# Inputs transposed by the DMA, and a convolution operand kept block by block, in a fused attention and state-space kernel

## The chip, the core and the metric

The kernel runs on one core of a Trainium2 chip. The core has five engines with queues of their own: TensorE (PE in the profile; PEld is its weight loads), VectorE (DVE), ScalarE (ACT), GpSimd (POOL) and SyncE (SP, which here only issues transfers). Sixteen DMA engines move data. The metric is the device time of one execution in microseconds.

## The reference

The inputs are x (2048 rows, 448 columns), the projections, and the parameters of a state-space layer (448 channels, 256 states), all in bf16. Two layers read the same x and a gate mixes them:

```python
q = (x @ wq).reshape(B, S, 16, 28).transpose(0, 2, 1, 3)
k, v = x @ wk, x @ wv                       # one K/V head for all 16 query heads
p = softmax(einsum("bhqd,bkd->bhqk", q, k) * 28**-0.5)
a = einsum("bhqk,bkd->bhqd", p, v) -> (B, S, 448) @ wo

dt = exp(log_dt)[:, None]                   # state-space layer, A, B, C complex
K[d, l] = Re( sum_n C[d,n] * exp(dt*A[d,n]*l) * dt*B[d,n] )      # l = 0..2047
b = causal convolution of x with K, per channel, + x * Dskip

g = sigmoid((x * gate_w).sum(-1, keepdims=True))
out = g * a + (1 - g) * b
```

## The kernel before

Every piece of work is an operation with an engine, an estimated duration, the data it reads and writes, and a priority `pr`. A planner (`Prog.schedule`, L158) simulates the engines with these estimates and fixes one order of instructions per engine; `emit` writes it out with semaphores. So each engine runs its list in order, and a wait at its head holds what stands behind it. `SLACK` (L87) is time that the planner adds before PE and DVE may use results of low-priority work. `dma` (L133) estimates transfers, and `pg.after` ties one operation behind another without a wait on its data.

**Loading and x.** x arrives in four blocks of 512 rows (`lx`, L505) in its row layout in `tab`. `prep_x` (L585) transposes each on PE with the identity (L597), 8 small matmuls for each half of the columns, and copies the result from PSUM to `xT`, one half by ACT (L607), one by DVE (L609). Contraction runs over 4 groups of 112 input channels (`DT = 112`); channel 4p+j stands on partition p in group j. K is projected (L615), evicted by ACT (L621), its absolute maximum taken by DVE (L624); V and the gate come from L631. The maximum over all keys (L640, "kap") goes into `Wb` (L642), which every query projection needs (`qproj`: L774, L780, L783, L786); it gives an upper bound of the scores in place of the softmax's running maximum. Blocks 1 to 3 of `xT` are stored to a scratch (XS, L636) and loaded back later (L789).

**Parameters.** `prep_params` (L686) transposes the six parameter arrays on PE (L713), then DVE forms products (L724), ACT sines and exponentials (L731, L732, L736, L739).

**Attention.** 16 steps of a block of 512 queries and 4 heads, each with 16 key tiles: scores on PE (L1125, or L1133 on masked copies of Q), exponentials on ACT (L1153) over two or three tiles of PSUM at a time, the product with V on PE (L1163) into one bank. `norm` (L1024) divides, `outp` (L1006) projects, `fold` (L1021) adds to the output in `O`.

**Convolution.** For 14 chunks of 32 channels DVE builds tables of powers (`masters` L795, `tables` L835); PE multiplies them into kernel taps (`kgen`, L898: two halves of 16 channels, a PSUM bank each), DVE adds Dskip (L926) and casts (L930) into `kstg`, POOL's queue stores the taps in a scratch in HBM (KP). SP's queue loads each group of four channels back as a Toeplitz tile of 1 MB (`tload`, L946) into one of seven places, three of which lie in `U` where its channels are used up. `conv` (L959) multiplies the tile with `U`: its weights are 32, 30, ... 18 columns of U (L974), four channels at a time on four column strips of the array. L984 multiplies with 1 - g, L995 brings the rows in order, L1003 adds to `O`. Two PSUM banks (5 and 7, `POOL` L85) are shared by taps, convolution, query and output projections.

**U.** `U` holds x for the convolution, channel by channel with 32 columns each. `loads` (L543 to L557) zeroes it all by a transfer, loads x rows into `O` in 16 transfers, POOL copies them into U in 8 instructions (L550), and one transfer copies half of U, shifted, within itself. Then `O` is zeroed (L560).

The last step (`norm(15)`, L1043, and `tail`, L1066) does the division by transposing with an fp32 identity (`identf`, which shares `msq`) and writes the output.

## Time and profile before

| | us |
|---|---|
| median of three runs (lowest, highest) | 521.37 (519.04, 526.63) |
| the profiled execution, its time | 521.35 |
| the profiled execution, its span | 519.4 |
| ACT busy | 483.6 |
| DVE busy | 447.5 |
| PE busy, weight loads | 431.1, 192.9 |
| POOL busy | 161.6 |
| first exponential (L1153) starts | 27.69 |
| first store of taps to KP | 93.6 |
| first Toeplitz load issued | 98.3 |
| last exponential ends | 504.17 |

The span runs from the first to the last instruction that the profile has; the execution's time has some 2 us around it. A line of groups gives line, engine, operation, tiles, count, then busy time and mean duration, then idle time before and what ended it. A line of the timeline gives start, duration, engine, line and what was done, then the idle time before it. Neighbouring instructions of one kind are merged into one line with a count.

### The profile page before, as it was taken

Reading aid. Unit: us, or ns where it says so; the run is one execution under the profiler, and the core shown is the slowest. Engines: PE = TensorE matmul, PEld = TensorE weight load, DVE = VectorE, ACT = ScalarE, POOL = GpSimd, SP = SyncE. Lnnn points to the kernel's source line nnn. Section 1 sums busy time; section 2 is a strip of 40 time slices with the busy share of each in tenths; the row PEclk is TensorE's granted clock in tenths of the full one; section 3 lists DMA queues with packets and bytes.
Section 4 is the critical chain, followed back from the end, with each engine's and each line's share of the span. In section 5 each row is a group of like instructions: output and inputs, shape, how many; then the busy total and the mean of one; then the engine's idle time right before and its main releaser. Section 6 shows DMA issues by size and latency. Waiting matters only on the chain.

```text
span 519.4 us, 18307 instructions
## 1 busy us (share of the span) xinstructions
PE 431.1 (83%) x8123; PEld 192.9 (37%) x8234; DVE 447.5 (86%) x798; ACT 483.6 (93%) x431; POOL 161.6 (31%) x299
## 2 busy tenths in 40 slices
PE   5778967888878789988878889988888889798884
PEld 4522111324334334434333434433344344443342
DVE  3877899999999999999999979999999989952123
ACT  3699899999999999999999999999999999899980
POOL 5014321612413442424214242432414233315100
PEclk9858587979999999999999999999999999999998
DMA  8995395497991998899998899899996999999996
GB/s 263 259 236 157 28 79 139 120 364 251 288 365 54 321 350 256 271 342 347 316 367 296 279 373 276 285 336 350 329 330 212 304 370 353 346 282 305 376 365 172
DMA packets 121997, 144.31 MB, mean 278 GB/s; under 512 B 53860, under 2 KB 60564, under 8 KB 121920
## 3 DMA queue, kind: packets, MB, share of 16 engines
q1 hardware_dynamic: 112368, 133.06, 81.3%
q0 software_dynamic: 8896, 9.53, 6.8%
q8 instruction: 64, 1.05, 0.8%
q10 hardware_dynamic: 656, 0.57, 0.4%
q14 instruction: 13, 0.11, 0.1%
HBM read 128.76 MB, written 5.23 MB: 258 GB/s over the span
## 4 chain that ended last, share of the span: by engine, by line
ACT 40%; DVE 36%; PE 17%; DMA 3%; issue 2%; ACTq 0%; SPq 0%
ACT expT L1153 40%; DVE tab L868 6%; PE psS L1133 4%; DVE tab L880 3%; DVE tab L879 3%; DVE tab L878 3%; PE psB L1163 3%; PE psS L1125 3%; DVE tab L890 3%; DVE tab L877 3%; DMA T<-KP_scratch 2%; DVE tmp L886 2%; DVE msq L811 1%; DVE cst L984 1%; PE psX L915 1%
## 5 line engine op out<-in xcount | busy, mean ns | idle before, releaser
L1153 ACT ACTIVATE expT<-psS 128x1536 bf16<-128x1536 f32 (+1 forms) x410 | 465.8, 1349 | 8.1 <-PE psS L1125 5.3
L1133 PE MATMUL psS<-qM,kT 128*128 128x512 bf16 x308 | 106.6, 402 | 35.5 <-ACT expT L1153 21.7
L1125 PE MATMUL psS<-qT,kT 29*128 29x512 bf16 x609 | 84.0, 401 | 27.8 <-ACT expT L1153 23.4
L1163 PE MATMUL psB<-expT,vaug 128*32 128x512 bf16 x1024 | 105.4, 403 | 1.1 <-ACT expT L1153 0.6
L137 POOL DMA_DIRECT2D KP_scratch<-kstg x112 | 62.3, 563 | 121.3 <-DVE kstg L930 114.6
L868 DVE TENSOR_TENSOR tab<-tab,mbf 128x512 bf16<-128x512 bf16 (+3 forms) x56 | 64.5, 1152 | 0.0
L1163 PEld LDWEIGHTS psB<-expT,vaug 128*32 128x32 bf16 x1024 | 26.2, 93 | 83.2 <-issue 78.7
L137 POOL DMA_DIRECT2D qM<-qT x64 | 32.0, 507 | 67.9 <-DVE qT L786 42.9
L1125 PEld LDWEIGHTS psS<-qT,kT 29*128 29x128 bf16 x609 | 20.1, 91 | 72.6 <-ACT expT L1153 60.2
L1133 PEld LDWEIGHTS psS<-qM,kT 128*128 128x128 bf16 x415 | 26.0, 98 | 54.8 <-ACT expT L1153 40.2
L137 POOL DMA_DIRECT2D rdenB<-R_scratch x60 | 30.5, 514 | 38.5 <-DMA R_scratch<-denT 27.9
L880 DVE TENSOR_TENSOR tab<-tab 128x128 bf16<-128x128 bf16 (+4 forms) x70 | 41.8, 597 | 0.0
L879 DVE TENSOR_TENSOR tab<-tab 128x128 bf16<-128x128 bf16 (+4 forms) x70 | 41.8, 597 | 0.0
L974 PE MATMUL psS<-T,U 128*32 128x128 bf16 (+7 forms) x1600 | 39.0, 220 | 2.2 <-DMA T<-KP_scratch 1.3
L974 PEld LDWEIGHTS psS<-T,U 128*32 128x32 bf16 (+7 forms) x1600 | 27.1, 94 | 18.1 <-issue 12.2
L137 POOL DMA_DIRECT2D denT<-acc x15 | 10.9, 726 | 69.1 <-DVE acc L1030 45.0
L890 DVE TENSOR_TENSOR tab<-tab,tmp 128x4096 bf16<-128x4096 bf16 x14 | 32.1, 2290 | 0.1
L878 DVE TENSOR_TENSOR tab<-tab,mbf 128x4096 bf16<-128x4096 bf16 x14 | 31.9, 2280 | 0.1
L877 DVE TENSOR_TENSOR tab<-tab,mbf 128x4096 bf16<-128x4096 bf16 x14 | 32.0, 2283 | 0.0
L974 PE MATMUL psX<-T,U 128*32 128x128 bf16 (+7 forms) x1216 | 29.9, 223 | 1.0 <-issue 0.9
L974 PEld LDWEIGHTS psX<-T,U 128*32 128x32 bf16 (+7 forms) x1216 | 21.0, 95 | 14.7 <-issue 11.3
L915 PE MATMUL psX<-tab 128*32 128x64 bf16 x1024 | 24.8, 241 | 1.1 <-DVE qT L786 0.4
(153 smaller groups left out, 517.1 us busy)
## 6 DMA issues: line engine op xcount, KB each, us to landing
T<-KP_scratch SPq DMA_DIRECT2D x176, 512.0 KB, 8.7
U<-KP_scratch SPq DMA_DIRECT2D x48, 512.0 KB, 9.6
rdenB<-R_scratch POOLq DMA_DIRECT2D x60, 64.0 KB, 5.7
U<-cst SPq DMA_DIRECT2D x1, 3584.0 KB, 18.7
qM<-qT POOLq DMA_DIRECT2D x64, 32.0 KB, 5.1
tab<-in_A_x_dram SPq DMA_DIRECT2D x4, 448.0 KB, 6.2
O<-in_A_x_dram SPq DMA_DIRECT2D x16, 112.0 KB, 2.7
O<-cst SPq DMA_DIRECT2D x1, 1792.0 KB, 28.6
```

The costliest lines, as they stand in the source:

```text
L137: return [e.dma_start(o, i, **kw) for o, i in pairs]
L868: vo(lambda e, dst=dst, src=src, mri=mri: e.tensor_tensor(dst, src, mri, ALU.mult), 4 * n, done + mk(lv), [kr, ki, tk])
L877: vo(lambda e, src=src, mi=mi, tv=tv: e.tensor_tensor(tv, src, mi, ALU.mult), 2 * n, done + mk(lv), [tk])
L878: vo(lambda e, dst=dst, src=src, mr=mr: e.tensor_tensor(dst, src, mr, ALU.mult), 2 * n, done + mk(lv), [kr, ki, ("gap", s)])
L879: vo(lambda e, dc=dc, tc=tc: e.tensor_tensor(dc[0], dc[0], tc[1], ALU.subtract), n, [tk, kr], [kr])
L880: vo(lambda e, dc=dc, tc=tc: e.tensor_tensor(dc[1], dc[1], tc[0], ALU.add), n, [tk, ki], [ki])
L890: vo(lambda e: e.tensor_tensor(tab.v(0, P, FM, [[4, 1024], [1, 4]]), tab.v(0, P, lo + 124, [[CG, 32], [-4, 32], [1, 4]]), rho.v(0, P, 0, [ ...
L974: r = e.matmul(ps.v(32 * j, 32 - 2 * n, 128 * k, [[1, 128]]), self.U.v(0, P, (4 * gi + j) * 32 + 2 * n, [[1, 32 - 2 * n]]), tbuf.v(0, P, t ...
L1125: r = e.matmul(self.psS.v(0, P, 512 * b, [[1, 512]]), kT.v(32 * h, DH + 1, 128 * kt, [[1, 128]]), qT.v(32 * h, DH + 1, 512 * (i % 2), [[1, ...
L1133: return e.matmul(self.psS.v(0, P, 512 * b, [[1, 512]]), kT.v(0, P, 128 * kt, [[1, 128]]), self.qM.v(0, P, (i % 2) * XQ + 512 * h, [[1, 51 ...
L1153: pg.op("act", lambda e: e.activation(expT.v(0, P, 512 * es[0], spread(es, n)), self.psS.v(0, P, 512 * bs[0], spread(bs, n)), AF.Exp, scal ...
L1163: r = e.matmul(self.psB.v(32 * h, 32, 0, [[1, 512]]), vaug.v(0, P, 32 * kt, [[1, 32]]), expT.v(0, P, 512 * ring[t], [[1, 512]]), start=(kt ...
```

## The change

It has five parts. x and the six parameter arrays are loaded by transposing transfers (`flip=True`), so that PE transposes neither. A group of contraction is now 128, 128, 128 and 64 consecutive channels (`KT`); the last 16 rows of the last 64 channels come by a transfer of single elements ("x4"), since a transposing read there would run past the end of x. The weights are loaded in rows to match, with the padding zeroed by three memsets on POOL. `U` is kept in four blocks of 128 channels (the last 64): a block holds 32 rows of x per partition, each with all of the block's channels side by side, and three plain transfers fill it; the weights of L974 step through it by 128 elements (64 in the last block). The taps of both halves of a chunk go to one bank and are evicted by one pair of instructions. `conv` issues the four loads of a chunk ahead of its matmuls. The fp32 identity for the gate has a place of its own (`idg`). Several transfers ("zO", "zW", "sk", "wo", "pad") join those that are held until the third store of x, the last six products of the parameters are put behind `Wb`, and the planner's slack for DVE goes from 1000 to 700 ns.

```diff
-    SLACK = {"pe": 500.0, "dve": 1000.0}
+    SLACK = {"pe": 500.0, "dve": 700.0}
+KT = (128, 128, 128, 64)
...
         def fn(e):
+            if flip:
+                return [e.dma_start_transpose(o, i) for o, i in pairs]
...
         def lx(q):
-            pg.dma([(self.xst.v(0, P, q * 4 * D, [[1, 4 * D]]), dram(x, q * 4 * P * D, [[4 * D, P], [1, 4 * D]]))],
-                   (128, 3584), f"x{q}", wr=[("xst", q)])
+            if q < 3:
+                pg.dma([(at(0, 4, 512), dram(x, r, [[D, 512], [1, 512]]))], (512, 1024), f"x{q}", wr=self.xk(q), flip=True, cost=1900)
+                return
+            pg.dma([(at(0, 3, 512), dram(x, r, [[D, 512], [1, 384]])),
+                    (at(1536, 1, 496), dram(x, r + 384, [[D, 496], [1, 128]]))],
+                   (512, 896), f"x{q}", wr=[("xT", q)], flip=True, cost=1900)
...
-            pg.dma([(raw.v(0, DT, k * 1024, [[1, 1024]]), dram(ins[names[k]], 0, [[1024, DT], [1, 1024]]))],
-                   (112, 2048), f"raw{k}", wr=[("raw", k)])
+            pg.dma([(raw.v(0, P, k * 1024, [[D, 2], [1, D]]), dram(ins[names[k]], 0, [[NM, D], [1, NM]]))],
+                   (448, 512), f"raw{k}", wr=[("raw", k)], flip=True, cost=900)
...
+        pg.dma([(xT.v(0, 64, xo + 2032, [[1, 16]]), dram(x, 2032 * D + 384, [[1, 64], [D, 16]]))],
+               (1024, 2), "x4", wr=[("xT", 4)], eng="act", slow=True)
...
-        self.late.append(pg.dma([(V0(self.U, 0, 32 * D, 64), Z(32 * D, 64))], (8192, 448), "zU", ...
-        for k in range(2):
-            ... 8 loads of x rows into O, 4 POOL copies O -> U
-        pg.dma([(half(rs + 16), half(0))], (28672, 32), "du", ...
+        for r in range(4):
+            w = min(128, D - 128 * r)
+            self.late.append(pg.dma(
+                [(part(r, 0, 16 * w, [[256, w // 16], [1, 256]]), self.cst.v(0, 64, 512, [[0, w // 16], [1, 256]])),
+                 (part(r, 0, 0, [[w, 16], [1, w]]), dram(x, 128 * r + 960 * D, [[D, 64], [-64 * D, 16], [1, w]])),
+                 (part(r, 1, 0, [[w, 32], [1, w]]), dram(x, 128 * r + 1984 * D, [[D, 64], [-64 * D, 32], [1, w]]))],
+                (3584, 2 * w), f"u{r}", rd=[("cst", 1)], wr=[("U", r)], pr=0.3).i)
...
         for q in range(4):
-            for hp in range(2):
-                ... 8 transposes on PE, then a copy PSUM -> xT by ACT (hp 0) or DVE (hp 1)
-            b = 4
+            b = q
...
         def trans(k, pr):
-            ... 8 transposes on PE into a bank of PSUM
+            return raw.v(0, P, k * 1024, [[D, 2], [1, D]]), ("raw", k)
+            if pr == 3:
+                pg.after[x.i] = self.kap + 1
...
+        G = self.grp()
         for q in range(2):
-            G = self.grp()
...
-                                G.v(32 * g, 32, 64 * k, [[1, 64]]),
+                                G.v(32 * g, 32, 256 * q + 64 * k, [[1, 64]]),
...
-        (for each half) tensor_tensor 4 columns, tensor_copy 4 x 63 columns, 4 stores
+        pg.op("dve", ... ko.v(0, P, 63, [[64, 8]]), G.v(0, P, 63, [[64, 8]]), ... rd=[X, "skt"], wr=["ksk"], pr=2)
+        pg.op("dve", ... tensor_copy(ko.v(0, P, 0, [[64, 8], [1, 63]]), G.v(...)), rd=[X], wr=["kst"], pr=2, unlock=G)
+        for q in range(2): 4 stores
...
         conv:
-                                     self.U.v(0, P, (4 * gi + j) * 32 + 2 * n, [[1, 32 - 2 * n]]),
+                                     self.U.v(0, P, uo + 2 * n * uw + j, [[uw, 32 - 2 * n]]),
```

## The prediction

> **What bounds the kernel now.** I read the busy shares first, then the groups, then time windows, then the timeline of the start and of the end.
>
> ```profile
> span 519.4 us, 18307 instructions
> PE 431.1 (83%) x8123; PEld 192.9 (37%) x8234; DVE 447.5 (86%) x798; ACT 483.6 (93%) x431; POOL 161.6 (31%) x299
> ...
> L1153 ACT ACTIVATE expT<-psS 128x1536 bf16<-128x1536 f32 (+1 forms) x410 | 465.8, 1349 | 8.1 <-PE psS L1125 5.3
> ```
>
> ACT's 410 exponentials take 465.8 us, with 8.1 us of idle time before them in all. No edit touches them. So the span is the time to the first exponential, plus a stream that is almost solid, plus what follows the last one. The windows give the slack of the others:
>
> ```profile
> 200.00:250.00 50.00, 44.98 (x912) 20.52 (x927) 49.62 (x101) 49.49 (x45) 16.59 (x30) 1.00 0.98 316
> 300.00:350.00 50.00, 45.44 (x928) 20.26 (x942) 45.88 (x79) 50.00 (x46) 19.36 (x36) 1.00 0.95 315
> 475.00:500.00 25.00, 21.25 (x505) 9.95 (x507) 4.10 (x8) 25.00 (x24) 3.52 (x7) 1.00 1.05 361
> ```
>
> The columns are PE, PEld, DVE, ACT and POOL busy, granted clock, DMA share, GB/s. In the middle ACT is full, DVE nearly so, and PE has about 5 us free in 50. Near the end DVE has 20 of 25 us free: it is close to the bound, but not what the end waits for.
>
> The start, from the timeline:
>
> ```profile
> 4.29 2.82 PE L597 MATMUL psS<-ident,tab 128*112 128x128 bf16 x24 [4.29 <-DMA tab<-in_A_x_dram]
> ...
> 22.52 0.67 ACT L621 ACTIVATE kT<-psS,small 128x512 bf16<-128x512 f32 x1
> ...
> 24.42 0.68 DVE L624 TENSOR_REDUCE small<-kT 128x1 f32<-128x512 bf16 x1
> ...
> 26.28 0.69 DVE L786 CAST qT<-psS 128x512 bf16<-128x512 f32 x1 [0.70 <-PE psX L713]
> ...
> 27.69 2.37 ACT L1153 ACTIVATE expT<-psS 128x1536 bf16<-128x1536 f32 x2 [0.40 <-PE psS L1125]
> ```
>
> The first exponential starts at 27.69: it needs the maximum over all of K, so all four blocks of x. The last block landed at about 12.1 (its issue starts near 2.66 and the longest landing of the four is 9.4). From there to 27.69, 15.6 us go into transposes on PE, evictions on ACT and DVE, and queueing among the parameter work.
>
> The end:
>
> ```profile
> 504.22 0.40 PE L1163 MATMUL psB<-expT,vaug 128*32 128x512 bf16 x4 [0.62 <-ACT expT L1153]
> ...
> 509.37 0.69 DVE L1063 TENSOR_TENSOR onT<-acc,psS 128x512 bf16<-128x512 f32 x1 [1.89 <-PE psS L1059]
> ...
> 511.99 0.68 DVE L984 TENSOR_TENSOR cst<-psS,omq 128x512 bf16<-128x512 f32 x1
> ...
> 514.01 0.42 DVE L1003 TENSOR_TENSOR O<-O,psS 128x256 bf16<-128x256 bf16 x1
> ```
>
> After the last exponential (504.17) come 15.2 us. The last convolution is in there too: L984 stands between the folds L1021, and L1003 is DVE's last instruction.
>
> **The start, part by part.** Gone are 64 transposes of x, their evictions (four of 1.02 us on ACT, four of 1.21 on DVE) and 48 transposes of parameters. What remains behind the last block of x is a chain of known rows: L615 x4 1.89 us on a cold clock (1.04 warm), L621 0.69, L624 0.68, L640 0.16, L642 0.25, L783 0.65, L786 0.69, L1125 0.66, and about 0.3 for hand-overs: 6.0 us.
>
> No transposing transfer is in the trace, so its landing is bounded. Ahead of the last block's end lie 2.10 MB of x (four blocks of 512 rows by 512 columns), 0.26 MB for the first parameter, and some 0.55 MB of plain loads. Below: plain rate. 5.31 MB moved in the first 20 us, with half-microsecond slices of about 330 GB/s, so 2.9 MB take 8.8 us; with 2.5 for start and receipt the last block lands at 11.3. Above: rows of 256 B as packets of their own. U<-U, 28,672 packets of 32 B in some 18.5 us on 16 engines, is 10.3 ns a packet; U<-cst, 8,192 of 448 B in 16.7 us, is 32.6; on the line between, 256 B cost 22.3 ns. Then 9,088 packets (4 x 2,048 and 896) take 12.7 us, the plain loads 3.2, and with 2.5 it lands at 18.4. Neither row is nearer in kind (one has the route, the other the packet), so I take the middle, 15: the first exponential at 21.0, **6.7 us earlier** (bounds 10.4 and 3.3).
>
> [...]
>
> Queues in the start. ACT issues ten DMAs instead of five; five occupied it from 0.81 to 3.14, so ten at 0.45 end near 5.4 and the table load (1.28) at 6.7, just when the first L615 could be done: hidden. If a ring backs up as for SP's KP_scratch<-cst issue (3.70 us), the first key eviction is late by 3 us, still ahead of the last. The 1,024 two-byte elements of x's corner cost 1,024 x 10.3 / 16 = 0.7 us beside the rest. POOL's three more memsets (0.1 to 0.3 each) push back the identity, which the start no longer waits for. The sine work (table loads 1.28 twice, L731 0.95, L732 1.03, L736 0.95: 5.5 us) fits into ACT's idle time before 17; if the last key eviction queues behind it, as before, that costs up to 2 us and is inside my bounds. Parameters 2 to 5 land 1.25 us apart by the same price, by 23; eight products of 1.08 follow, so DVE's squarings start near 31 instead of 40.07.
>
> **U, and DVE's lead.** POOL's eight copies (8.8 us) go. Beside them DVE's small instructions stretched: between 47 and 57 us eight of them took 0.95 to 1.58 us (8.8 in sum) where the same shapes take 0.29 (2.3): 6.4 us back. SP loses U<-cst, 16 loads and U<-U (18.7 and 20.5 us to landing) and gains twelve transfers: 12,288 rows of 256 B at 22.3 ns are 17 us of the engines, plus some 1 MB of zeros, now with O<-cst, Wo and the pad behind the third store of x. All that should land by about 55 to 60; before, SP was held by O<-cst until 76 and issued the first T load at 98.3. Cost nothing, covered by the first table, which DVE ended at 87.9.
>
> Per chunk two evictions L930 (0.41) and L926 (0.17) become one of 504 columns (0.69, as L786) and one of 0.18: 1.16 to 0.87, 14 times, 4 us. With 9 us at the start, 6.4 and 4, DVE's last table (L895 at 463.3) comes 15 to 20 us earlier, while ACT is only 6.7 earlier: convolution gains on attention. Against it, the taps of the first half can't be stored before the second half is done (92.8 to 98.2: 5.4 us a chunk), and SP waited 67.3 us for these stores; that is less than DVE's lead, and without the lead it would stand in the end, 5 us. One bank held longer can delay a projection; L774 made DVE wait 5.9 us in all.
>
> **The end.** With the last convolution done before the last exponential, its pieces leave the tail: L984 0.68 and L1003 0.42, **1.1 us**. If it is not done, nothing. The fp32 identity in its own place drops a dependence on msq; the copy L1196 (0.18) stays: nothing.
>
> **The middle** is planned anew, with another slack constant; ACT's 8.1 us of idle can halve or grow by half: 0, plus or minus 4.
>
> **Sum.** 519.4 - 6.7 - 1.1 = 511.6 of span; the profiled execution took 521.35 with 2.0 around its span, so 513.5. The median of the runs is 521.37, the same.
>
> **Rivals.**
>
> *Convolution weights read in steps (slower).* U's columns now lie 128 elements apart (64 in the last block). The row for steps is L915's: four elements apart, 32 columns load in 117 ns, where L974's 32 contiguous ones take 97.
>
> ```profile
> L915 PEld LDWEIGHTS psX<-tab 128*32 128x32 bf16 x1024 | 19.1, 117 | 11.4 <-issue 6.3 <-DVE tab L895 1.4 <-DVE O L1021 0.6
> ...
> L597 PEld LDWEIGHTS psS<-ident,tab 128*112 128x112 bf16 x64 | 7.3, 204 | 5.2 <-DMA tab<-in_A_x_dram 4.3 <-issue 0.7
> ...
> L974 PEld LDWEIGHTS psS<-T,U 128*32 128x32 bf16 x200 | 5.5, 97 | 6.8 <-issue 3.7 <-DMA T<-KP_scratch 1.6 <-DVE O L1003 0.5
> ```
>
> L597, 112 columns in the same step, takes 204: (204 - 117) / 80 = 1.09 ns a column. For it to cost time the loads of the four column strips must not overlap. At step four they do: 38 matmuls of L915 in 0.74 us are 13.5 ns each, against 12.6 for L974 (28 in 0.56). If at step 128 they came one behind the other, 25 columns would be 27 ns, 14.7 more on 3,584 matmuls: 53 us. PE's 5 us free in 50, over 448 convolution matmuls, are 11 ns each: it decides from 24 ns a matmul on, and half of the 53 would show: 513.5 + 26 = 540. [...]
>
> *Transfers no faster than the transposes they replace.* If the last block lands at 21.7 (2.9 MB at 150 GB/s), the start gives nothing and the tail 1.1: 520. At 100 GB/s it is 530. For it: small packets were slow here (U<-cst). Against: plain loads at 330.
>
> *More than I count.* Landing at 11.3 gives 10.4; ACT's idle time halved, 4; the tail 1.1: 506. For it: DVE's lead, and PE free of 48 transposes in the first exponentials.
>
> **Chances.** Forecast (508 to 517) 0.46, more 0.24, slow transfers 0.19 (one in ten of them over 530), stepped weights 0.11. The range leaves out most of the stepped weights and the far ends of the others: 504 to 529. Measurement tells about 2% from no change, that is 510.9 and 531.8: faster takes the third rival and the forecast's lower edge, 0.30; slower 0.12; within, 0.58.
>
> **What would show it.** First exponential at 21 (17.3 to 24.4); L615 on each block right behind its landing; DVE's squarings from 31; kstg's first eviction near 80 instead of 92.8; ACT's idle time before L1153 near 8; L974's spacing at 12 to 14 ns; no L984 behind the last L1153. I am wrong if the squarings start no earlier, if ACT waits for PE in the middle, or if ACT's queue holds the early evictions.

## The result

The changed kernel takes 585.62 us (median of four runs, 581.81 to 588.27), the kernel before 521.88 beside it (519.04 to 526.63): a ratio of 1.121, 95% interval 1.110 to 1.131. It is slower by an eighth; forecast was 513.5.

From the page of the changed kernel, the same three lines as before (L1149 is the exponential now):

```profile
span 582.9 us, 18025 instructions
...
PE 465.4 (80%) x8009; PEld 232.8 (40%) x8122; DVE 493.3 (85%) x766; ACT 536.6 (92%) x427; POOL 160.0 (27%) x297
...
L1149 ACT ACTIVATE expT<-psS 128x1536 bf16<-128x1536 f32 (+1 forms) x410 | 522.6, 1476 | 11.4 <-PE psS L1121 6.7
```

ACT's idle time grew by only 3.3 us. What grew is the exponentials themselves: the same 410 instructions, 465.8 us before and 522.6 now. DVE has 32 instructions less and is busy for 46 us more.

The time windows of the changed kernel, two in the middle and one ahead of its end (columns as shown before):

```profile
200.00:250.00 50.00, 42.99 (x751) 21.47 (x750) 49.20 (x83) 47.24 (x37) 14.95 (x28) 0.97 0.62 191
300.00:350.00 50.00, 40.64 (x830) 21.57 (x842) 50.00 (x75) 48.77 (x38) 16.25 (x27) 1.00 0.74 239
535.00:560.00 25.00, 21.24 (x402) 10.19 (x402) 3.68 (x7) 24.16 (x22) 3.25 (x6) 0.93 1.05 366
```

ACT is still nearly full, but 50 us hold 37 and 38 of its instructions where they held 45 and 46. PE has more time free than before, 7 to 9 us instead of 5, so it did not become the bound. The groups with the shapes kept apart say which instructions became longer; first two of the kernel before, then those of the changed kernel:

```profile
L1153 ACT ACTIVATE expT<-psS 128x1536 bf16<-128x1536 f32 x205 | 320.0, 1561 | 6.7 <-PE psS L1125 5.3 <-PE psS L1133 0.9
...
L877 DVE TENSOR_TENSOR tab<-tab,mbf 128x4096 bf16<-128x4096 bf16 x14 | 32.0, 2283 | 0.0
```

```profile
L1149 ACT ACTIVATE expT<-psS 128x1536 bf16<-128x1536 f32 x205 | 356.4, 1739 | 8.6 <-PE psS L1121 6.7 <-PE psS L1129 0.9
...
L869 DVE TENSOR_TENSOR tab<-tab,mbf 128x4096 bf16<-128x4096 bf16 x14 | 40.2, 2873 | 0.0
...
L907 PEld LDWEIGHTS psX<-tab 128*32 128x32 bf16 x1152 | 21.2, 118 | 13.6 <-issue 9.1 <-DVE qT L779 1.1 <-DVE tab L887 0.8
...
L970 PEld LDWEIGHTS psX<-T,U 128*32 128x32 bf16 x184 | 10.7, 199 | 4.5 <-issue 2.8 <-DVE O L999 0.7 <-DVE tmp L878 0.4
```

The large exponential went from 1561 to 1739 ns, the table product L869 from 2283 (as L877) to 2873, the convolution's load of 32 weight columns (L970) from 97 (as L974) to 199. The loads of the taps (L907) are as before, 118 ns to 117. A stretch of the timeline shows such a longer instruction and what runs beside it:

```profile
103.80 1.43 DVE L815 TENSOR_TENSOR msq<-seedw,seedz 128x512 f32<-128x512 bf16 x1
104.06 0.97 PEld L970 LDWEIGHTS psX<-T,U 128*32 128x32 bf16 x32
104.28 0.90 PE L970 MATMUL psX<-T,U 128*32 128x128 bf16 x32
```

The same product took 0.68 us on average in the kernel before (as L823); here it lies beside 32 convolution matmuls and takes 1.43.

The start of the changed kernel, from its timeline:

```profile
2.31 5.94 SPq L138 DMA_TRANSPOSE T<-in_A_x_dram  x1
...
14.27 0.13 PEld L615 LDWEIGHTS psS<-T,expT 128*128 128x128 bf16 x2 [6.19 <-DMA T<-in_A_x_dram]
...
20.15 0.62 DVE L557 COPY Wq<-mbf 128x1792 bf16<-128x1792 bf16 x1
...
20.82 0.33 PEld L767 LDWEIGHTS psX<-xT,Wq 128*128 128x128 bf16 x3 [2.94 <-DVE Wq L557]
...
22.41 0.13 PEld L615 LDWEIGHTS psS<-expT 128*128 128x128 bf16 x2 [0.44 <-issue]
...
26.21 0.26 DVE L642 TENSOR_SCALAR Wb<-expT,small 128x128 bf16<-128x128 bf16 x1
...
27.02 2.73 PE L631 MATMUL psB<-expT 128*128 128x29 bf16 x32
...
29.68 0.11 PEld L776 LDWEIGHTS psX<-qT,Wb 128*128 128x128 bf16 x1
...
32.70 1.45 ACT L1149 ACTIVATE expT<-psS 128x1536 bf16<-128x1536 f32 x1 [1.23 <-PE psS L1121]
```

The first exponential starts at 32.7: 5.0 us later than before, not 6.7 earlier. The second block of x is first used at 14.27, 12 us behind the start of its issue. The last load of x is issued at 15.27 and landed at 19.17 by the trace; the keys of the last block come at 22.41, and 10.3 us follow.

The end, from the timeline:

```profile
573.48 0.68 DVE L980 TENSOR_TENSOR cst<-psX,omq 128x512 bf16<-128x512 f32 x1
...
577.37 0.68 DVE L980 TENSOR_TENSOR cst<-psS,omq 128x512 bf16<-128x512 f32 x1
...
578.60 0.42 DVE L999 TENSOR_TENSOR O<-O,psS 128x256 bf16<-128x256 bf16 x1 [0.55 <-PE psS L991]
```

The last exponential is done at 567.75. Two convolutions (L980) stand behind it now, where one stood.

For everything below I split each span into four terms that add up to it (to 0.1 us of rounding): the start of the first exponential; ACT's idle time from there to the start of the last one; what is left between these two, **ACT's own work**; and the rest, the tail. The idle time here is smaller than the page's, 7.7 instead of 8.1 and 10.2 instead of 11.4, because the page also counts the wait just ahead of the first exponential, which is in the first term. Before: 27.7 + 7.7 + 467.9 + 16.1 = 519.4. After: 32.7 + 10.2 + 524.2 + 15.8 = 582.9. Of the 63.5 us, 56.3 are ACT's own work, 5.0 the start, 2.5 waits; the tail is 0.3 shorter.

### The profile page after: what moved, and what is told of

Read it like the earlier page. It is cut to its first block, busy times and chain, and to the rows that moved or that the text cites. A ratio compares the mean times of both kernels' runs of the same rounds, so it can differ in the third digit from the quotient of the medians.

```text
span 582.9 us, 18025 instructions
## 1 busy us (share of the span) xinstructions
PE 465.4 (80%) x8009; PEld 232.8 (40%) x8122; DVE 493.3 (85%) x766; ACT 536.6 (92%) x427; POOL 160.0 (27%) x297
## 3 DMA queue, kind: packets, MB, share of 16 engines
q8 instruction: 63, 1.03, 0.7%
## 4 chain that ended last, share of the span: by engine, by line
DVE 65%; ACT 18%; PE 13%; DMA 2%; issue 1%; SPq 0%; ACTq 0%
ACT expT L1149 18%; DVE tab L860 10%; DVE tab L871 6%; DVE tab L872 6%; DVE tab L869 6%; DVE tab L882 5%; DVE tab L870 5%; DVE tmp L878 4%; DVE msq L803 3%; PE psS L1129 2%; DMA T<-in_A_x_dram 2%; DVE cst L980 2%; PE psS L1121 2%; PE psB L1159 2%; DVE seedz L807 2%; DVE onT L1036 2%
## 5 line engine op out<-in xcount | busy, mean ns | idle before, releaser
L1149 ACT ACTIVATE expT<-psS 128x1536 bf16<-128x1536 f32 (+1 forms) x410 | 522.6, 1476 | 11.4 <-PE psS L1121 6.7
L139 POOL DMA_DIRECT2D KP_scratch<-kstg x112 | 64.9, 634 | 59.7 <-DVE kstg L922 59.7
L860 DVE TENSOR_TENSOR tab<-tab,mbf 128x512 bf16<-128x512 bf16 (+3 forms) x56 | 71.4, 1274 | 0.0
L1159 PEld LDWEIGHTS psB<-expT,vaug 128*32 128x32 bf16 x1024 | 26.1, 93 | 83.3 <-issue 76.7
L970 PE MATMUL psX<-T,U 128*32 128x128 bf16 (+6 forms) x1472 | 51.5, 259 | 0.2 <-DVE O L999 0.2
L970 PEld LDWEIGHTS psX<-T,U 128*32 128x32 bf16 (+6 forms) x1472 | 45.7, 200 | 14.2 <-issue 11.7
L871 DVE TENSOR_TENSOR tab<-tab 128x128 bf16<-128x128 bf16 (+4 forms) x70 | 48.5, 692 | 0.0
L970 PE MATMUL psS<-T,U 128*20 128x128 bf16 (+7 forms) x1344 | 47.8, 257 | 0.6 <-DVE kstg L922 0.3
L139 POOL DMA_DIRECT2D qM<-qT x64 | 33.3, 527 | 52.4 <-DVE qT L779 51.5
L970 PEld LDWEIGHTS psS<-T,U 128*18 128x18 bf16 (+7 forms) x1344 | 42.2, 196 | 13.1 <-issue 10.5
L872 DVE TENSOR_TENSOR tab<-tab 128x128 bf16<-128x128 bf16 (+4 forms) x70 | 47.4, 677 | 0.0
L139 POOL DMA_DIRECT2D rdenB<-R_scratch x60 | 31.4, 529 | 43.4 <-DMA R_scratch<-denT 33.4
L869 DVE TENSOR_TENSOR tab<-tab,mbf 128x4096 bf16<-128x4096 bf16 x14 | 40.2, 2873 | 0.0
L870 DVE TENSOR_TENSOR tab<-tab,mbf 128x4096 bf16<-128x4096 bf16 x14 | 37.4, 2669 | 0.1
L882 DVE TENSOR_TENSOR tab<-tab,tmp 128x4096 bf16<-128x4096 bf16 x14 | 37.1, 2652 | 0.1
L907 PE MATMUL psX<-tab 128*32 128x64 bf16 x1152 | 26.9, 242 | 2.5 <-issue 1.0
```

Of the source, the lines that this page charges most:

```text
L139: return [e.dma_start(o, i, **kw) for o, i in pairs]
L860: vo(lambda e, dst=dst, src=src, mri=mri: e.tensor_tensor(dst, src, mri, ALU.mult), 4 * n, done + mk(lv), [kr, ki, tk])
L869: vo(lambda e, src=src, mi=mi, tv=tv: e.tensor_tensor(tv, src, mi, ALU.mult), 2 * n, done + mk(lv), [tk])
L870: vo(lambda e, dst=dst, src=src, mr=mr: e.tensor_tensor(dst, src, mr, ALU.mult), 2 * n, done + mk(lv), [kr, ki, ("gap", s)])
L871: vo(lambda e, dc=dc, tc=tc: e.tensor_tensor(dc[0], dc[0], tc[1], ALU.subtract), n, [tk, kr], [kr])
L872: vo(lambda e, dc=dc, tc=tc: e.tensor_tensor(dc[1], dc[1], tc[0], ALU.add), n, [tk, ki], [ki])
```

## Experiments: the step of the weight reads

Theory: PE reads the convolution's weight columns from U at a distance of 256 B (128 B in the last block, 16 of the 112 groups of four channels), and that lengthens what ACT and DVE do at the same time. In the first six runs only the distance is changed, in the changed kernel or in the one before. The convolution then multiplies other elements of U, and its part of the output is not the reference's; the instructions and the shapes stay.

Run 1, step of one element in the changed kernel:

```
-            uw = min(128, D - 4 * gi // 128 * 128)
+            uw = 1
```

> The changed kernel with one edit: the weights of L970 are read with a step of one element instead of 128 (64 in the last block), so the convolution multiplies with other elements of U and its part of the output is not the reference's; instructions, orders and transfers stay. Theory A (the stepped weight reads lengthen the instructions of ACT and DVE that run beside them): the 410 exponentials go back from 522.6 to about 466 us, DVE's L872 from 677 to about 597 ns, and the time from 585 to about 528 (the first exponential stays at 32.7, 5 later than before). Rival B (something else that the change moved lengthens them, such as the new places of x or the transfers beside them): exponentials stay above 510 us and the time above 575. Rival C (PE itself is late through long weight loads): exponentials stay near 1476 ns, idle time before them falls from 11.4 us.

Run 2, the kernel before with the steps of the changed one (128 elements, 64 in the last block):

```
-   self.U.v(0, P, (4 * gi + j) * 32 + 2 * n, [[1, 32 - 2 * n]]),
+   self.U.v(0, P, <block and column as in the change> + j, [[min(128, D - 4 * gi // 128 * 128), 32 - 2 * n]]),
```

> The kernel before with one edit: the weights of L974 are read with a step of 128 elements (64 in the last block) instead of one, so the convolution multiplies with other elements of U. Theory A: exponentials grow from 465.8 to about 522 us, L880 from 597 to about 680 ns, the time from 521 to about 578. Rival B: no change, 521.

Runs 3 and 4, in the changed kernel:

```
-            uw = min(128, D - 4 * gi // 128 * 128)
+            uw = 4                                               # run 3
+            uw = min(100, 60) if 4 * gi // 128 == 3 else 100     # run 4
```

> The changed kernel with a step of 4 elements (8 bytes) in the weights of L970 (other elements of U are multiplied). [...] If what costs is a step that is a multiple of 64 bytes or more, a return to the same place of the memory (theory A2): as with step one, near 528, with loads of 117 ns.

> The changed kernel with a step of 100 elements (200 bytes; 60 in the last block) in the weights of L970 (other elements of U are multiplied). [...] Theory A2 (steps that return to the same place, powers of two): near 528, weight loads shorter than the 200 ns of step 128.

Measured: before 522.33; step 1 531.85 (ratio 1.018, 1.012 to 1.024); step 4 531.86 (1.017, 1.008 to 1.025); step 100 532.06 (1.017, 1.010 to 1.024); and the kernel before with step 128 575.89 (1.101, 1.093 to 1.109). One number in an access pattern is worth 54 us in both kernels. The groups by shape of the kernel before with step 128:

```profile
L1153 ACT ACTIVATE expT<-psS 128x1536 bf16<-128x1536 f32 x205 | 361.1, 1762 | 4.1 <-PE psS L1125 2.8 <-PE psS L1133 0.6
...
L868 DVE TENSOR_TENSOR tab<-tab,mbf 128x4096 bf16<-128x4096 bf16 x14 | 40.3, 2876 | 0.0
...
L974 PEld LDWEIGHTS psS<-T,U 128*32 128x32 bf16 x200 | 11.8, 201 | 4.4 <-issue 3.0 <-DVE O L1003 0.8 <-DVE tab L849 0.4
```

and of the changed kernel with step 100:

```profile
L1149 ACT ACTIVATE expT<-psS 128x1536 bf16<-128x1536 f32 x205 | 314.0, 1532 | 7.5 <-PE psS L1121 6.0 <-PE psS L1129 0.9
...
L860 DVE TENSOR_TENSOR tab<-tab,mbf 128x4096 bf16<-128x4096 bf16 x14 | 32.1, 2290 | 0.0
...
L970 PEld LDWEIGHTS psX<-T,U 128*32 128x32 bf16 x184 | 6.6, 134 | 7.7 <-DMA T<-KP_scratch 3.1 <-issue 3.1 <-DVE O L999 0.7
```

Step 100 is the run that decides between "a large step" and "this step": its loads are almost 40% longer than contiguous ones (134 ns to 97), yet exponentials and tables are as short as with step 1. The lateness of PE, which my rival had priced, isn't it: in the kernel before with step 128 ACT stood idle for less time than without it (5.4 us to 7.7).

Runs 5 and 6 asked how near to 256 B the cost lies:

```
-            uw = min(128, D - 4 * gi // 128 * 128)
+            uw = 64                                              # run 5
+            uw = min(96, 60) if 4 * gi // 128 == 3 else 96       # run 6
```

> The changed kernel whose convolution reads its 32 weight columns 64 elements (128 B) apart instead of 128 (256 B); it multiplies other elements of U, the number of instructions and their shapes stay. Theory A, the cost follows how few places within 256 B the columns return to: 256 B returns to one place, 128 B to two, so about half of the 54 us between 585.6 and 531.9 would be gone: 552 to 565 us, exponentials near 1620 and 1165 ns. Rival A1, any step that is a power of two costs the whole: near 586 us, exponentials 1739 and 1216. Rival A2, only 256 B and its multiples collide: 532 us, exponentials 1540 and 1115.

> The changed kernel with a step of 96 elements (192 B, four places within 256 B), 60 in the last block; other elements of U are multiplied. Theory A by places: a quarter of the excess, 540 to 548 us. Theory that only 256 B and its multiples collide: 532 us, exponentials 1540 and 1115. [...]

Measured 535.54 (ratio 1.026, 1.018 to 1.033) and 532.37 (1.020, 1.015 to 1.025). Half of the distance doesn't cost half: with 128 B ACT's own work is 2 to 3 us more than in the other runs of the changed kernel, with 192 B nothing. My graded theory fell, and the 64 B that the expectation of run 3 names is not the measure either: 128 and 192 B are multiples of it. What is left, among the steps tried, is a cost of 256 B, nearly alone.

Run 7 keeps the whole computation and lengthens the rows of U's blocks by four unused elements, so that the columns lie 264 B apart (136 in the last block):

```
+PAD = 4
+UP = 32 * (128 + PAD)
...
-            uw = min(128, D - 4 * gi // 128 * 128)
-            uo = 4 * gi // 128 * TW + 4 * gi % 128
+            uw = min(128, D - 4 * gi // 128 * 128) + PAD
+            uo = 4 * gi // 128 * UP + 4 * gi % 128
```

The transfers that fill U and the places of T in it follow the new distance; the room comes from packing the parameters' landing place closer.

> The changed kernel with its whole computation kept and only the rows of U's blocks lengthened by 4 unused elements (264 B instead of 256, 136 instead of 128 in the last block), so the same weights are read with another step. If the step of 256 B is the whole of what the block-wise U cost: 530 to 533 us (ratio 1.015 to 1.021), exponentials near 1540 and 1115 ns, tables near 2290 instead of 2652 to 2873; the rest to the kernel before is the late first exponential (some 5 us) and ACT's waits. If 8 B beyond 256 is too near the same place: 555 to 586 us.

Measured 532.57 (ratio 1.019, 1.012 to 1.025), as expected. All seven in one table, ns for a load of 32 columns and us for the four terms:

| run | step, B | load | start | idle | ACT's work | tail | span |
|---|---|---|---|---|---|---|---|
| before | 2 | 97 | 27.7 | 7.7 | 467.9 | 16.1 | 519.4 |
| 1 | 2 | 96 | 33.3 | 10.9 | 468.3 | 17.0 | 529.5 |
| 3 | 8 | 109 | 32.8 | 13.0 | 469.0 | 17.1 | 531.8 |
| 5 | 128 | 168 | 32.7 | 16.1 | 471.6 | 15.8 | 536.3 |
| 6 | 192 | 138 | 32.7 | 13.5 | 468.9 | 15.7 | 530.8 |
| 4 | 200 | 134 | 32.1 | 12.5 | 469.1 | 16.6 | 530.3 |
| 7 | 264 | 142 | 33.2 | 14.0 | 469.9 | 16.1 | 533.2 |
| after | 256 | 199 | 32.7 | 10.2 | 524.2 | 15.8 | 582.9 |
| 2 (before) | 256 | 201 | 26.1 | 5.4 | 526.4 | 16.3 | 574.2 |

The column of ACT's work separates two rows from seven. Each row is one profiled execution, and the executions of one kernel lie several us apart (the kernel before: 519.04 to 526.63). The 54 us are far beyond that; differences of a few us of idle time between two rows are not. What is left of the change without that step is 10 to 14 us of span (17 with 128 B): some 5 of the start, and 3 to 6 of ACT's idle time. The next runs are about these.

## Experiments: U and taps alone, with the start of before

Run 8 is the kernel before with U block by block (rows of 264 B, plain transfers) and the taps of a chunk in one bank; x and the parameters still go through TensorE.

```
-        self.late.append(pg.dma([(V0(self.U, 0, 32 * D, 64), Z(32 * D, 64))], ... "zU" ...
-        (16 loads, 8 POOL copies, "du")
+        (four blocks as in the change, rows of w + PAD)
...
+        G = self.grp()          # one bank for both halves of a chunk
         for q in range(2):
-            G = self.grp()
```

> The kernel before with two parts of the change alone: U block by block filled by plain transfers (rows lengthened by 4 elements as in the run above) and the taps of a chunk in one bank; x and the parameters are still transposed by TensorE, the fp32 identity stays where it was. Theory: the 9.5 us that the changed kernel loses beside the step come from its start, and these two parts are neutral or a little to the good, since the squarings lose the POOL copies beside them: 516 to 523 us (ratio 0.99 to 1.003), first exponential at 27 to 28 us. Rival: taps in one bank or the block-wise U also make ACT wait for PE in the middle: 526 to 531 us with ACT's idle time before the exponentials at 11 us or more instead of 8. If 264 B collides as 256 does: above 550.

Measured 531.19 (ratio 1.018, 1.014 to 1.022), outside the 516 to 523 of the theory. The terms, of the profiled execution, the shortest of its five: 27.7 + 4.3 + 468.0 + 26.0 = 526.0. ACT waited less, where the rival had it wait more, and its last exponential was done at 500.6; but the tail is 10 us longer. Its timeline:

```profile
496.39 4.23 ACT L1159 ACTIVATE expT<-psS 128x1536 bf16<-128x1536 f32 x4 [0.17 <-PE psS L1131]
...
516.30 1.08 PE L980 MATMUL psX<-T,U 128*32 128x128 bf16 x32 [1.66 <-DMA T<-KP_scratch]
...
518.91 1.08 PE L980 MATMUL psX<-U 128*32 128x128 bf16 x32 [1.52 <-DMA U<-KP_scratch]
...
521.48 0.42 DVE L1009 TENSOR_TENSOR O<-O,psX 128x256 bf16<-128x256 bf16 x1 [0.75 <-PE psX L1001]
```

The last convolution takes one matrix T after the other as it lands, 2.6 us apart. The 28 convolutions read 112 of these, 1 MB each, and between 440 and 450 the transfers ran at 118 GB/s: SP waited for PE, most of all for convolutions (162 us in the whole run), to free places for T (the order on PE had the last taps (445 to 453) in front of convolution 22). The stores of taps were not late: DVE's last eviction of taps was at 453.4, 19 us earlier than before.

Run 9 changes nothing but the planner's allowance behind DVE, and with it the written order. Run 11 has the taps in halves as before, so of the change U alone.

```
-    SLACK = {"pe": 500.0, "dve": 1000.0}
+    SLACK = {"pe": 500.0, "dve": 550.0}     # run 9; run 11: 500.0
```

> The run of the kernel before with the block-wise U (rows of 264 B) and the taps in one bank, where the planner's allowance behind DVE is set from 1000 to 550 ns, so that the order written out puts the last convolutions earlier; nothing else differs. In the run without it the exponentials ended at 500.6, 3.7 us ahead of the kernel before, and the last convolution came 25.4 us behind them instead of 15.2, waiting for loads of T. Theory: that tail was the written order: exponentials end at 500 to 502, tail 15 to 16, span 515 to 518, time 517 to 520 us (ratio 0.991 to 0.997). Rival: the loads of T into U's freed blocks can't come sooner whatever the order: tail 22 to 26 us again, 527 to 531 us.

> The kernel before with the block-wise U alone (rows of 264 B, plain transfers), taps in halves as before, allowance behind DVE 500 ns. Against the run with the taps in one bank and 550 ns it tells what the taps are worth: 14 evictions of 0.67 and 0.19 us instead of 28 of 0.41 and some 0.2 leave DVE some 5 us freer, which should not reach the end while ACT sets it. Theory: within 2 us of that run, 516 to 520 us. If the taps in one bank cost (a bank held longer): 3 us or more below it; if they gain: 3 us or more above it.

Measured: run 9 526.38 (ratio 1.009, 1.004 to 1.013), terms 27.6 + 8.6 + 468.5 + 15.9 = 520.6 in its profiled execution, which was the shortest of its ten; run 11 526.41 (1.006, 1.003 to 1.010), 29.0 + 12.7 + 468.8 + 16.2 = 526.7. The tail of run 8 was the order: it is back at 15.9. But what the earlier convolutions take from the tail they give back in the middle: ACT's idle time rose from 4.3 to 8.6. So the expected 517 to 520 was missed, and so was the 516 to 520 for run 11: the two parts together gain nothing. Between taps in one bank (run 9) and two (run 11) no difference in time is seen; the allowance differs by 50 ns too, so the taps are not quite alone in it.

## Experiments: the start

The plan that orders the work has x's blocks cost 1.9 us each, and its own first exponential comes at 21.6, near my forecast; the chip's came at 32.7. Run 10 is run 7 with the planner told other costs, and with its allowance behind DVE at 400 ns instead of 700:

```
-    (512, 1024), f"x{q}", wr=self.xk(q), flip=True, cost=1900)
+    (512, 1024), f"x{q}", wr=self.xk(q), flip=True, cost=(3000, 6500, 3000)[q])
...
-    (512, 896), f"x{q}", wr=[("xT", q)], flip=True, cost=1900)
+    (512, 896), f"x{q}", wr=[("xT", q)], flip=True, cost=3500)
...
-    (448, 512), f"raw{k}", wr=[("raw", k)], flip=True, cost=900)
+    (448, 512), f"raw{k}", wr=[("raw", k)], flip=True, cost=1400)
```

> The changed kernel with lengthened rows of U, and its planner told what the transposing loads took in its trace (x 3.0, 6.5, 3.0 and 3.5 us, a parameter 1.4, instead of 1.9 and 0.9), its allowance behind DVE 400 ns instead of 700: the instructions are the same, the written order differs. Theory: beside the step, the loss is a late start and an order that was written for a first exponential at 21.6 us and met one at 33: ACT's idle time before the exponentials falls from 15.2 to 5 to 9 us, first exponential at 30 to 33, tail near 15 to 16, time 521 to 525 us. Rival: ACT waits for PE because of what the parts are (taps in one bank, block-wise U), whatever the order: idle time 13 us or more, 528 to 532 us.

Measured 526.63 (ratio 1.006, 1.002 to 1.010), terms 31.1 + 11.0 + 467.5 + 15.8 = 525.4: 6 us better than run 7, but above the 521 to 525 of the theory. With the wait ahead of the first exponential, as the expectation counts it, ACT's idle time fell from 15.2 to 11.0, where 5 to 9 were expected. Which of the two settings did it was not tried.

Run 12 meant to bring q's projection and three quarters of the V matmuls ahead of x's last block; run 13 forces what run 12 did not reach. The lines below leave out the costs that the planner is told: in run 12 those of run 10 with 2.0 us for x's last block, in run 13 1.9 and 0.9 us again, with 1.5 to 9.0 us more until the loads land. The allowance is 500 and 400 ns.

```
+    (the five loads of ACT's queue) cost=100                     # run 12
+            if i == 0:
+                pg.after[self.mv3.i] = len(pg.ops) - 2           # V of the last block behind the bias of q
```


```
+        pg.after[<copies of Wv>] = <copy of Wq>
...
+            if pr == 0.2:
+                pg.after[x.i] = self.wvg      # first parameter product behind the weight copies
-            if pr == 3:
+            if pr in (1, 3):
                 pg.after[x.i] = self.kap + 1
```

> The changed kernel with lengthened rows of U, written in another order at the start: the planner is told the measured times of the transposing loads and that the small loads of ACT's queue land early, so that the copies of Wq and Wv, the first projection of q and the V matmuls of the first three blocks of x come ahead of the last block, and the V matmuls of the last block are held behind the first projection; allowance behind DVE 500 ns. The instructions are the same. Theory: the last block of x lands at 19 to 20 us whatever the order, and from there the chain is 6 to 7 us (keys 2.0, copy and maximum 1.4, the small steps 0.4, bias and copy of q 1.3, QK and hand-overs 1): first exponential at 26 to 27.5 us instead of 33 and 31, idle time 9 to 13 us, tail 16, time 521 to 524 us (ratio 0.997 to 1.003). Rival: the loads themselves hold the start and the order at PE and DVE doesn't: first exponential at 30 us or later, 526 us.

> As the run before, which meant to bring the small work ahead of the last block of x and did not: on DVE the copy of Wq still stood behind the first parameter product and ran at 19.9, so q's first projection, and behind it the keys of the last block, ran at 20.6 and 22.6, and the V matmuls of three blocks at 24.5 to 28.5. Here the order is forced: the first parameter product stands behind the copies of Wq and Wv, and the parameter work that follows the sines behind the maximum of the keys; allowance behind DVE 400 ns. The instructions are the same. Theory that the order made the start late: keys of the last block right behind their landing, at 18.5 to 20.5; first exponential 6 to 7 us later, at 25 to 27.5; time 520 to 523 us. Rival that the landing made it: the keys of the last block run at 22 us or later although PE and DVE are free, first exponential at 28.5 or later, 525 us or more. What ACT does before its first exponential in the kernel before comes behind it here and takes some 3 us of the gain back in both.

Measured: run 12 527.36 (1.009, 1.006 to 1.012), first exponential 31.9, idle 10.6; run 13 529.90 (1.014, 1.006 to 1.021), 31.9 + 9.2 + 470.4 + 15.7 = 527.2. In run 12 DVE's copy of Wq still ran at 19.94, behind the first parameter product. In run 13 it ran at 13.84, and this is the start that followed:

```profile
17.48 1.40 PE L636 MATMUL psB<-expT,xT 128*128 128x29 bf16 x16 [0.97 <-DVE expT L563]
...
18.82 2.00 PE L620 MATMUL psS<-T,expT 128*128 128x512 bf16 x4
...
25.34 2.00 PE L620 MATMUL psS<-expT 128*128 128x512 bf16 x4
...
31.86 1.45 ACT L1160 ACTIVATE expT<-psS 128x1536 bf16<-128x1536 f32 x1 [0.62 <-PE psS L1132]
```

PE now works without a break from 17.5 to 27.4 and is itself what is late: 2.00 us for the four matmuls of a block's keys and 1.40 for 16 V matmuls. Before, the same took 1.03 and 0.55 from 14 us on (1.89 and 0.63 ahead of that). The times are those that the rivals gave, but not for their reason: by the traces the last load of x had landed at 18.64 in run 12 and at 19.45 in run 13, 3.9 and 5.9 us before its keys ran, and in run 13 PE was not free. So these starts did not wait for the landing: the order on DVE and PE held them in run 12, the order and the pace of PE in run 13.

On the pace: in run 13 the 512-column matmuls of keys (L620) and scores (L1132) take 601 to 634 ns each from 6.1 to 38.1 us, while the windows show a granted clock of 1.00. The views show 1.00 also where a trace has no record of it. In the kernel before the record begins with 1.00 at 13.0 us; its 512-column matmuls take 608 to 634 ns up to 9.9 us and fall from 587 to 380 at 13.0; where 0.50 is recorded (23.3 to 40.4) they take 602 to 634 again. The slow pace of run 13 is that of the half clock, and its mean clock, 0.972 over 527.2 us, leaves room for 29.5 us at 0.50, less than the 32 us of slow pace from 6.1 to 38.1: the granted clock of 1.00 that the next expectation names is no measured one. Nor is there a record for the "cold clock" of the prediction's chain, at 8.63 us. (The expectation also counts 192 transposes in the kernel before; there are 64 of x and 48 of the parameters.)

Runs 14 and 15 add 80 and 104 transposes of the identity into an unused bank, while PE waits for x, to runs 13 and 10:

```
+                def dummy(e):
+                    for k in range(8):
+                        r = e.matmul(w.v(0, P, wo + 128 * k, [[1, 128]]), self.ident.v(0, P, 0, [[1, P]]),
+                                     self.ident.v(0, P, 0, [[1, P]]), is_transpose=True, tile_position=(0, 0))
```

> The run before (forced order at the start) with 80 transposes of the identity by TensorE added into an unused bank while PE waits for x; what is computed stays. In that run PE's first matmuls stayed slow up to the first exponential, 603 to 634 ns for 512 columns and 196 for the V matmuls, at a granted clock of 1.00, where the kernel before, with its 192 transposes of x and the parameters, ran them at 378 and 175 ns from 14 us on. Theory: the transposes that the change removes had kept PE busy and thereby at its faster pace; with PE kept busy again the matmuls of keys, V and q fall to about 380 and 175 ns, PE's stretch from 17.5 to 27.4 us shrinks by 4 to 5 us, first exponential at 26 to 28.5 us instead of 31.9, time 524 to 527 us instead of 529.9. Rival: they stay at 600 ns or the added work stands in the way: first exponential at 31 us or later, 529 us or more.

> The run planned with the measured loads (first exponential 31.1 us, 526.6 us), allowance behind DVE 450 instead of 400 ns, with 104 transposes of the identity by TensorE added while PE waits for x; what is computed stays. Theory that a busy PE keeps its faster pace: keys, V and q at about 380 and 175 ns; the four matmuls of q's first projection (21.7) and of the last block's keys (23.6) take 1.0 us less each and the V matmuls 1 us less ahead of the bias, so the first exponential comes at 28 to 29.5 us; 523 to 525 us, level with the kernel before within 0.5%. Rival: no faster, or held by the added work: first exponential at 31 us or later, 526 us or more.

Measured: run 14 526.96 (1.005, 1.000 to 1.010), first exponential 33.4; run 15 526.39 (1.006, 1.002 to 1.009), 31.2. The time of run 14 lies in the range of its theory by luck: its start is 1.5 us later than that of run 13, and it is ACT's idle time that is shorter, 5.1 us instead of 9.2. From the timeline and the windows of run 15:

```profile
18.77 1.13 PE L617 MATMUL psS<-expT 128*128 128x512 bf16 x4
...
23.80 2.02 PE L617 MATMUL psS<-expT 128*128 128x512 bf16 x4
```

```profile
16.00:20.00 4.00, 4.00 (x50) 2.80 (x49) 2.54 (x5) 1.21 (x3) 0.00 (x0) 1.00 1.29 215
...
24.00:28.00 4.00, 4.00 (x33) 2.04 (x30) 2.92 (x8) 2.40 (x4) 0.00 (x0) 0.50 0.95 227
```

The first half of the theory holds: with PE kept busy the keys of the third block took 1.13 us instead of 2.00. The second half fell: from 24 us on the granted clock is 0.50, and the keys of the last block take 2.02 again. The kernel before has the same half clock, from 23.3 to 40.4 us, but by then it had the keys of all four blocks (the last at 19.44). In run 14 it came already at 15.2. The first recorded stretch of full clock lasted 10.2 us in the kernel before (13.0 to 23.3) and 3.4 us in the changed kernel (17.8 to 21.2). That PE is kept busy doesn't prolong it by itself: run 14 was at 0.50 from 15.2 to 28.8, and between 16 and 28 PE was busy for at least 1.78 of every 2 us. What ends these stretches was not found. In run 15 the last load of x had landed at 21.37, before the half clock came (23.8), but PE waited until 22.50 for DVE's copy of Wq and ran q's projection first, and the keys of the last block came just behind its end.

## Why the prediction was wrong

**The exponentials.** The step that failed is a sentence of the first paragraph: of ACT's 410 exponentials, "No edit touches them". From it the sum took their 465.8 us over unchanged. No edit changes an instruction of ACT; but the step of the weight reads lengthens them, ACT's own work by 56.3 us, and DVE's 4096-column table products by 11 to 26%. Runs 1, 2, 4 and 7 show it. None of the three signs of being wrong that the prediction names covers this.

**The rival "stepped weights"** had the right place and sign and a wrong price. It reckoned PE late from 24 ns a matmul on and 540 us for it. The spacing did grow towards that (28 matmuls in 0.67 us are 24 ns, 32 in 0.90 are 28; divided the same way, 28 in 0.56 were 20 before, and the 12.6 of the prediction is from start to start), but ACT's wait for PE grew by 3 us. It had no term for what one engine's reads do to another's, and with that 0.11 was too little. The loads did grow with the step (109 ns at four elements, 134 to 142 at 96 to 132), the time not with them: 192, 200 and 264 B cost ACT nothing (468.9 to 469.9 us of its own work, 468.3 at 2 B). And ACT and DVE slow down when only PE's reads change: from the kernel before to run 2 ACT's own work went from 467.9 to 526.4 us and the table product L868 from 2285 to 2876 ns.

**The start** was forecast 6.7 us earlier and came 5.0 later. The 11.7 us between 21.0 and 32.7 are three parts. First the landing, 15 in my sum: the last load of x was there at 19.17, 4.2 late and beyond the 18.4 of my upper bound. The transfers of the first 22 us, in the answer on the DMA queues of the changed kernel and of the one before:

```profile
DMA packets 15160, 3.58 MB, mean 163 GB/s; under 512 B 14584, under 2 KB 15160, under 8 KB 15160
```

```profile
DMA packets 4299, 5.78 MB, mean 263 GB/s; under 512 B 2544, under 2 KB 2672, under 8 KB 4298
```

With 16 engines in use from 2 to 22 these make about 21 ns a packet, most of them (11,768) of 256 B: the price of my upper bound, 22.3, was about right, and the middle that I took was the mistake. The 2.5 us for start and receipt in both bounds was my estimate, which no run shows as such; what the kernel before shows is 1.0 us from the first issue (0.81) to the first packet (1.83). A landing at 19.17 and my chain of 6.0 would still have given 25.2, 2.5 us ahead of the kernel before; the rest is PE's. Next, 3.2 us until PE came to the last keys at 22.41, behind a projection of q that waited for DVE's copy of Wq, which I had not in the chain. Last, the chain of 6.0 took 10.3: 64 V matmuls at the slow pace (24.35 to 29.75) held L776 for 3.2, and the next projection held QK for 1.0. I had looked for what queues on ACT there, and not on PE.

**DVE's lead** came: taps were evicted last at 450.9 to 453.4 in runs 1, 7 and 8 instead of 472.4, 19 to 21 us earlier, where I had 15 to 20. It bought nothing: run 8 turned it into 3.4 us less waiting and lost 10 in the tail. First taps came at 84.1 (forecast 80). The squarings came at 34.8 (forecast 31); the 40.07 that the prediction gives for them before is a cast (L831), and the first squaring (L811) stood at 45.67.

**The end** did not give its 1.1 us; the tail is 15.8 for 16.1. **The middle**, 0 plus or minus 4, was 2.5 and in run 7 6.4. Run 10, another written order, took 3.0 of that away; the rest stays open.

**Transfers no faster** forecast 520 to 530; the kernel without its 256 B takes 526 to 533. The transfers were as slow as it said (163 GB/s, where it took 150), but the last block landed at 19.17 and not at its 21.7, so that by my chain of 6.0 the start would still have been earlier than before.

No version here beats the kernel before; the best are 0.5 to 0.9% slower (runs 9, 10, 11, 12, 14, 15).

## What to carry to other kernels

Before an operand is laid out anew, look at the distance in bytes between the elements that one instruction takes from a partition, and stay off 256 B: ACT's own work was 524 us with it and 470 with 264 B, four unused elements per row. An engine that is full can be slowed by another's accesses (ACT by 58 us in run 2), so "no edit touches it" is an argument about its instructions, not about its time; ask what its neighbours now read, and watch the mean duration of instructions that were not changed. When small packets are priced from rows, take the price for their size (22.3 ns for 256 B in the prediction, about 21 measured), not the middle between it and the rate of larger ones. And when a transfer seems late, compare its landing with the first instruction that uses it: here the keys of the last block came 3.2 us behind it.

## What the runs showed of the hardware

- Weight loads of TensorE whose columns lie 256 B apart lengthen the work of ACT and DVE beside them: ACT's own work 468 to 524 us (changed kernel) and 526 (run 2), DVE's four 4096-column products take 2536 to 2873 ns (changed kernel) and 2725 to 3085 (run 2) instead of 2280 to 2290. With 2, 8, 192, 200 and 264 B nothing of it is seen (467.9 to 469.9 us; 2280 to 2290 ns), with 128 B 2 to 3 us (471.6). Which of ACT's and DVE's accesses are held up (reads, writes, SBUF or PSUM on ACT's side), and whether 512 B does the same, was not tried; DVE's table products have all their operands in SBUF (`tab`, `mbf`, `tmp`).
- The load of 32 columns itself took 97, 109, 138, 134, 142, 168 and 200 ns at 2, 8, 192, 200, 264, 128 and 256 B.
- At the start PE's 512-column matmuls took 587 to 634 ns until the trace's first record of a granted clock of 1.00, at 13.0 us (before) and 17.8 (changed kernel), and 377 to 390 ns behind it. After 10.2 and 3.4 us the clock fell to 0.50 for 17.1 and 23.9 us, and the matmuls took 601 to 634 ns again. With transposes added, four such matmuls took 1.14 us at 14.16 (run 14) instead of 2.00 at 14.52 (run 13), and 1.13 at 18.77 (run 15) instead of 2.00 at 17.02 (run 10), though in run 13 PE worked without a break from 17.5 to 27.4 and stayed at 603 to 631 ns.
